# First 512 tokens of a fused attention and MLP block in pairs of token tiles, row maxima sent from ScalarE's queue, output loads spread, scratch of q and k in two parts

## The chip, the cores and the metric

The kernel runs on one core of a Trainium2 chip. The metric is device time in microseconds of one execution, the median over runs. A core has a matrix engine (TensorE, PE in the profile), VectorE (DVE), ScalarE (ACT), GpSimd (POOL) and SyncE (SP), each with an instruction queue of its own that it works off in order, and 16 DMA engines, for which the queues of SP, ScalarE and GpSimd can issue transfers.

## What is computed

The reference adds an attention block and a gated MLP to the input, both fed by the same layer norm of x. There are 2048 tokens of width 512, 32 heads of width 16, and a hidden width of 2 x 896. Everything is float32.

```python
def _A_ref(x, wqkv, wo):
    qkv = (x @ wqkv).reshape(B, S, 3, H, Dh).transpose(2, 0, 3, 1, 4)
    q, k, v = qkv[0], qkv[1], qkv[2]
    scores = jnp.einsum("bhqd,bhkd->bhqk", q, k) * (Dh ** -0.5)
    p = _softmax(scores, axis=-1)
    o = jnp.einsum("bhqk,bhkd->bhqd", p, v)
    return o.transpose(0, 2, 1, 3).reshape(B, S, D) @ wo

def _B_ref(x, w_in, w_sp, b_sp, w_out):
    z = _gelu(jnp.einsum("bsd,df->bsf", x, w_in))
    z1 = z[..., :Fh]
    z2 = _layernorm(z[..., Fh:], axis=-1)
    g = jnp.einsum("ts,bsf->btf", w_sp, z2) + b_sp[None, :, None]
    return jnp.einsum("bsf,fd->bsd", z1 * g, w_out)

xn = _layernorm(x, axis=-1)
return x + _A_ref(xn, wqkv, wo) + _B_ref(xn, w_in, w_sp, b_sp, w_out)
```

## The kernel before

**Numbers in two parts.** Every factor of a float32 product is kept as a high part, rounded to the reduced format fp32r, and a low part, the rest. `mm3` (L161) makes a product of three matmuls, high x high, low x high and high x low, at lines L162 to L164. `split` (L157) makes the parts of an input: ScalarE copies it to the rounded high part (`act`, L55; its instruction is L57 for every copy, exponential and tanh that goes through it), VectorE subtracts that from the input (L159). Weights are fetched by `begin` (L168) and split by `end` (L182). By default GpSimd makes both parts, at L187 and L188. With `early`, which only the preamble uses, GpSimd's own queue loads the weight a second time, straight into the tile of the high part (L179), and VectorE makes the low part (L185).

**Layout.** `x` comes in four chunks `g` of 512 tokens, each of four token tiles of 128. `load_x` (L223) fetches a chunk as two tiles of 128x1024, each holding a pair of token tiles. `norm_x` (L233) is a generator: VectorE takes statistics of each token tile (L244, L245), ScalarE the root of the variance (L247), VectorE the reciprocal and the shift, and ScalarE scales each token tile (L253); with `parts=2` it does the chunk in two halves. `turn_x` (L255) transposes a chunk on PE (L259), four 128x128 blocks for each of the four blocks `c` of the model width, into a PSUM tile of the tag `s`, of which there are three; then it splits that into `xnT[g, c]` and stores it to DRAM for later stages. The tags `d` and `o` of PSUM have one tile each and hold the products.

**Preamble (L816 to L855).** Before the steady loop the instructions are issued in the written order. `x` of chunk 0, the weights of q and k for the first eight heads (`w0`, called wqk0_0 and wqk0_1), `x` of chunk 1 and the four blocks of the weights of v (`wv`) are loaded; chunk 0 is normalized and turned whole. Then, for each chunk, `qk_group` (L287) makes q and k of the first heads (24 products), `load_stacks` (L598) loads them back from DRAM, and `v_tile` (L334) makes v for the chunk's four token tiles (12 products each); the next chunk's normalization and transposes are put between these. So chunk 0's order is 16 transposes, q, k, v0 to v3.

**q and k through DRAM.** `qk_split` (L305) splits a block of q or k, and `qk_store` (L278) writes it to `qscr` or `kscr` in three parts for 512 tokens: for q high, low, high, for k high, high, low, so that one part is written twice, in two DMAs of 512 KB and 256 KB. `load_stacks` then copies the three parts of 16 rows each of a head in one DMA to 48 partitions of `qst` and `kst`, which puts the three products of scores into one matmul of 48 rows. There are 16 pairs `p` of heads, `NP`; `qst` and `kst` have two buffers, used in turn.

**Steady loop.** A counter `half` runs in half-steps. A step is three attention tiles `b`, `b + 1`, `b + 2` of 128 keys by 512 queries for two heads: `scores` (L903 is its matmul) fills a PSUM tile of tag `s`, `exp` on ScalarE (tile `pf`, of which there are `PF` = 6) makes the probabilities, and `pv` multiplies them with v (L877) into the tag `o`. `LEAD` = 27 tiles ahead of it the row maxima are made: `max_mm` (L630) computes scores of queries by keys, `max_red` (L638) reduces them on VectorE, and once per 16 tiles `max_fin` (L641) ends the maximum of 512 queries: VectorE transposes it into `ms` (L657), SP sends `ms` to DRAM (`mscr`), and four DMAs bring it back as rows of `qst`, so that the score matmul subtracts the maximum itself. There are 64 such maxima. `half` starts at -18, so that the first nine steps, the lead-in, have maxima only; attention starts at `b` = 0.

**Background work.** PE's remaining time is filled from `queue`: the rest of q and k, the second half of the hidden layer (`z2_all`) with its layer norm on GpSimd, the first half (`z1_all`), the product over tokens (`spatial`), the output of the MLP (`mlp_out`, L564, which loads two parts of the hidden product, `hp`, and a tile of `x`, `xr`, one token tile ahead) and the output of attention (`attn_out`). A `credit` (L993) says how many ns of background products may be issued at the end of a half-step: 2600 in each half-step of the lead-in, four products of three matmuls; from `b` = 0 on, in odd half-steps only, a share of the work that is left.

**Queues and delays.** `move` (L100) issues a DMA from SP. `later(k, ...)` keeps a call for `k` half-steps, and `flush` issues what is due at the head of a half-step. `store` issues at once from GpSimd's queue in the preamble and through `later` on SP in the steady loop. An estimate of when GpSimd will be free, `pool[0]` (L110 to L123), in a time of 2.7 us per half-step, decides when a generator goes on after work on GpSimd (`pool_done`); whatever is given to GpSimd adds to it, the preamble's work too. Buffers are tiles of a pool that are used in turn; a DMA into a buffer, or out of one, stands at the head of its queue until its data are there.

## Time and profile before

| | us |
|---|---|
| runs of the kernel before | 1963.83, 1964.72, 1965.18 (median 1964.72) |
| the profiled execution | 1965.23 |
| its span, first to last instruction | 1963.1 |
| busy: TensorE (PE) | 1933.9 (99%) |
| busy: VectorE | 1372.9 (70%) |
| busy: ScalarE | 1231.7 (63%) |
| busy: GpSimd | 720.9 (37%) |

The span is what the trace covers; the time of the profiled execution has 2.13 us beside it. The engines' busy times overlap. Mean granted clock of TensorE over the span was 0.997 of full speed. A row of the order of time has the start in the span, the duration (of one instruction, or from the first to the last of a run of like ones), the engine, the line, the operation, the output and input tiles with their sizes, and, in brackets, the engine's idle time just ahead of it and what ended it. A row of a group has the line, the engine, the operation and the count, then least, median and greatest ns of one, then the first and last start. A row of a stretch has its bounds and length, then each engine's busy time with its count of instructions. A row of the waits has the engine with the waiting instruction, the engine and instruction that ended the waits, and their sum, count and longest in us.

### The profile page before, as it was taken

To read this page: it belongs to the slowest core of one execution; us is meant where nothing else is said; L and a number is where in the kernel's file an instruction comes from. 1 tells how busy PE (TensorE), PEld (TensorE's weight loads), DVE (VectorE), ACT (ScalarE), POOL (GpSimd) and SP (SyncE) were. 2 spreads that over 40 slices of the span, in tenths; PEclk is the share of its full clock that TensorE was granted. 3 is DMA by queue.
4 is the path that set the end of the run, shared out by engine and by line. 5 is a ranking of instruction groups with operands and counts; after the bars stand their busy time and mean duration, and the time that the engine had idled before them with its cause. 6 is when DMAs were issued, how large, how long until landed. Compare 5 with 4: busy or idle time off the path is not lost.

```text
span 1963.1 us, 32545 instructions
## 1 busy us (share of the span) xinstructions
PE 1933.9 (99%) x12544; PEld 1047.0 (53%) x12544; DVE 1372.9 (70%) x1562; ACT 1231.7 (63%) x1402; POOL 720.9 (37%) x787
## 2 busy tenths in 40 slices
PE   7999999999999999999999999999999999999998
PEld 6765555555555555555555555555555555555543
DVE  5256777777777677777777777777777777777872
ACT  4336778888777665656666665665566655556664
POOL 2234368789776931026122531017112300002100
PEclk9999999999999999999999999999999999999999
DMA  9586444363535645365545744346364645355323
GB/s 327 204 292 200 139 107 122 108 176 111 154 117 159 187 123 140 91 162 159 151 138 154 211 129 125 108 126 204 105 163 135 176 142 145 106 152 154 105 73 113
DMA packets 234195, 294.20 MB, mean 150 GB/s; under 512 B 34536, under 2 KB 134520, under 8 KB 231160
## 3 DMA queue, kind: packets, MB, share of 16 engines
q1 hardware_dynamic: 229816, 282.08, 49.4%
q0 software_dynamic: 4224, 10.04, 1.4%
q8 instruction: 99, 1.62, 0.3%
q14 instruction: 56, 0.46, 0.1%
HBM read 190.09 MB, written 101.97 MB: 149 GB/s over the span
## 4 chain that ended last, share of the span: by engine, by line
PE 91%; DVE 3%; POOL 2%; DMA 2%; ACT 1%; issue 1%; SPq 0%; DVEq 0%; POOLq 0%; ACTq 0%
PE o L877 23%; PE mx L630 15%; PE st L903 15%; PE sp L162 7%; PE sp L164 5%; PE sp L163 5%; PE mo L162 2%; PE z1p L162 2%; PE qk L162 1%; DVE mm L638 1%; PE mo L163 1%; PE mo L164 1%; PE z2p L162 1%; PE z1p L164 1%; PE z1p L163 1%; PE qk L163 1%
## 5 line engine op out<-in xcount | busy, mean ns | idle before, releaser
L638 DVE TENSOR_REDUCE mm<-mx 128x2 f32<-128x1024 f32 x1024 | 1221.5, 1222 | 501.3 <-PE mx L630 497.2
L57 ACT ACTIVATE pf<-st 128x1024 f32<-128x1024 f32 x1024 | 1028.7, 1025 | 621.9 <-PE st L903 597.2
L877 PE MATMUL o<-pf,vall 128*32 128x512 f32 (+1 forms) x5120 | 511.0, 513 | 0.0
L630 PE MATMUL mx<-kst,qst 48*128 48x512 f32 x2048 | 446.9, 434 | 3.1 <-DVE mm L638 2.0
L903 PE MATMUL st<-qst,kst 50*128 50x512 f32 x2048 | 445.6, 432 | 1.5 <-DVE mm L638 1.4
L630 PEld LDWEIGHTS mx<-kst,qst 48*128 48x128 f32 x2048 | 192.0, 185 | 268.7 <-ACT pf L57 168.6
L903 PEld LDWEIGHTS st<-qst,kst 50*128 50x128 f32 x2048 | 193.3, 185 | 164.0 <-issue 85.7
L877 PEld LDWEIGHTS o<-pf,vall 128*32 128x32 f32 x5120 | 131.4, 109 | 233.7 <-issue 211.7
L162 PE MATMUL sp<-wsp,zs 128*128 128x512 f32 x448 | 193.8, 433 | 0.3 <-DVE z1i L549 0.2
L556 POOL TENSOR_TENSOR z1i<-z1i,hhl 128x512 f32<-128x512 f32 x28 | 36.0, 1286 | 425.9 <-DVE z1i L549 422.4
L164 PE MATMUL sp<-wsp,zs 128*128 128x512 f32 x448 | 175.9, 393 | 0.0
L163 PE MATMUL sp<-wsp,zs 128*128 128x512 f32 x448 | 175.9, 393 | 0.0
L162 PEld LDWEIGHTS sp<-wsp,zs 128*128 128x128 f32 x448 | 83.9, 187 | 68.9 <-issue 52.1
L164 PEld LDWEIGHTS sp<-wsp,zs 128*128 128x128 f32 x448 | 84.1, 188 | 19.3
L163 PEld LDWEIGHTS sp<-wsp,zs 128*128 128x128 f32 x448 | 84.4, 188 | 12.2
L187 POOL CAST wo<-wo0r 128x512 fp32r<-128x512 f32 x1 | 0.6, 611 | 191.4 <-DMA wo0r<-in_wo 191.4
L310 POOL TENSOR_TENSOR qkhl<-qr,qkhl 128x512 fp32r<-128x512 f32 x24 | 30.9, 1289 | 78.9 <-ACT qkhl L57 78.8
L162 PE MATMUL z2p<-w,xt 128*128 128x448 f32 x128 | 51.3, 401 | 0.0
L162 PE MATMUL mo<-wout,hp 128*128 128x512 f32 x112 | 48.5, 433 | 0.6 <-DVE xr L593 0.4
L691 POOL TENSOR_TENSOR ob<-ob 128x512 f32<-128x512 f32 (+1 forms) x16 | 20.6, 1288 | 77.0 <-DMA ob<-rscr 54.5
L164 PE MATMUL z2p<-w,xt 128*128 128x448 f32 x128 | 46.9, 366 | 0.0
L163 PE MATMUL z2p<-w,xt 128*128 128x448 f32 x128 | 46.8, 365 | 0.0
(378 smaller groups left out, 1974.8 us busy)
## 6 DMA issues: line engine op xcount, KB each, us to landing
zs<-z2scr SPq DMA_DIRECT2D x112, 512.0 KB
escr<-e SPq DMA_DIRECT2D x60, 256.0 KB
hscr<-hhl SPq DMA_DIRECT2D x28, 512.0 KB
qst<-qscr SPq DMA_DIRECT2D x30, 384.0 KB
kst<-kscr SPq DMA_DIRECT2D x30, 384.0 KB
xscr<-xnT POOLq DMA_DIRECT2D x16, 512.0 KB, 6.0
qscr<-qkhl SPq DMA_DIRECT2D x16, 512.0 KB
kscr<-qkhl SPq DMA_DIRECT2D x16, 512.0 KB
```

Source lines behind the costliest of these rows:

```text
L57: return nc.scalar.activation(out, in_, func, **kw)
L162: nc.tensor.matmul(acc, lh, rh, start=first, stop=False)
L163: nc.tensor.matmul(acc, ll, rh, start=False, stop=False)
L164: nc.tensor.matmul(acc, lh, rl, start=False, stop=last)
L187: gps(0.6).tensor_copy(t[:, 0, :n], rw[:, :n])
L310: gps(1.3).tensor_sub(hl[:, 1, :], src, hl[:, 0, :].bitcast(F32))
L556: gps(1.3).tensor_add(z1, z1, hl[:, 1, :].bitcast(F32))
L630: nc.tensor.matmul(acc[:, j, :], qst[p % 2][rows, tt * P:(tt + 1) * P], kst[p % 2][rows, kc * 512:(kc + 1) * 512], start=True, stop=True)
L638: dve(1024).tensor_reduce(mmax[i // 16][:, :, t, kc], mstep.pop(i), AX.X, ALU.max)
L691: gps(1.3).tensor_mul(both[rows, 0, :], both[rows, 0, :], both[rows, 2, :])
L877: nc.tensor.matmul(acc[cols:cols + VW, a:a + w], vpack(kt - 1 + r, 2 * p + j), pf[:, j * 512 + a:j * 512 + a + w], start=(kt == 1 and a == ...
L903: nc.tensor.matmul(st[:, j, :], kst[p % 2][rows, kt * P:(kt + 1) * P], qst[p % 2][rows, c * 512:(c + 1) * 512], start=True, stop=True)
```

## The change

*The start.* `x` of chunk 0 is loaded as four DMAs of one token tile each. The weights of v come next, then those of q and k, then chunks 1 and 2 of `x`. GpSimd's second loads of the weights are gone (`early` now chooses only the buffer). For wv0 and wv3 ScalarE copies the high part and VectorE subtracts; wv1, wv2 and `w0` are split by GpSimd. `norm_x` yields between its two halves, and `turn_x` takes a range of token tiles: tiles 0 and 1 are turned first (eight transposes in one go, then four splits of half width), then v0 is made, and v1 turns tiles 2 and 3 after its sixth product through `mid`; v2 and v3 follow. Chunk 1 is normalized between these tiles. q and k of chunk 0 come after its v instead of before, and chunk 1 is turned right after the first q. In later chunks too `turn_x` issues all 16 transposes before the first split, with blocks 0 and 3 sharing one PSUM tile. A root of `epst` on ScalarE, whose result is overwritten, stands first.

*GpSimd's estimate* is set back to -1000 at the end of this part, so the work given to GpSimd until then no longer counts.

*Maxima.* `ms` is sent to DRAM by ScalarE's queue instead of SP's, right after the exponentials of the next half-step, through the list `behind`; the four row loads stay on SP, two half-steps after the transpose.

*Output loads.* In `mlp_out` the two `hp` loads are issued one and two half-steps later and `xr` three, except for the first token tile.

*Scratch.* `qscr` and `kscr` keep two parts, for q high and low, for k low and high, stored by one DMA of 512 KB; `load_stacks` takes the three parts of a head with two DMAs, one of two parts and one of the third.

*Credit.* At `b` = 0 each half-step in which no product with v was issued gets the credit of the lead-in, 2600.

```diff
-    qscr = [dr.tile([P, 3, S], F32, name=f"qscr{m}") for m in range(4)]
-    kscr = [dr.tile([P, 3, S], F32, name=f"kscr{m}") for m in range(4)]
+    qscr = [dr.tile([P, 2, S], F32, name=f"qscr{m}") for m in range(4)]
+    kscr = [dr.tile([P, 2, S], F32, name=f"kscr{m}") for m in range(4)]
     xscr = [[dr.tile([P, 2, 512], F32, name=f"xscr{g}_{c}") for c in range(ND)] for g in range(NG)]
...
+    def soon(k, fn, *args):
+        fn(*args)
+
     def flush():
...
         rw = t512(nm + "r") if early == "t" else big.tile([P, 512], F32, tag="raw", name=nm + "r", bufs=3)
-        dst, hi = rw[:, :n], t[:, 0, :n]
+        dst = rw[:, :n]
         if blocks > 1:
             src = src.rearrange("(c p) f -> p c f", p=P)
-            dst, hi = (v.rearrange("p (c f) -> p c f", c=blocks) for v in (dst, hi))
+            dst = dst.rearrange("p (c f) -> p c f", c=blocks)
         move(dst, src)
-        if early:
-            nc.gpsimd.dma_start(hi, src)
         return t, rw, n
-    def end(loaded, early=False):
+    def end(loaded, low=None, high=False):
         t, rw, n = loaded
-        if early:
-            nc.vector.tensor_sub(t[:, 1, :n], rw[:, :n], t[:, 0, :n].bitcast(F32))
+        if high:
+            low.tensor_sub(t[:, 1, :n], rw[:, :n], t[:, 0, :n].bitcast(F32))
+        elif low:
+            nc.scalar.activation(t[:, 0, :n], rw[:, :n], AF.Copy)
+            low.tensor_sub(t[:, 1, :n], rw[:, :n], t[:, 0, :n].bitcast(F32))
         else:
...
         for i in range(len(xt)):
-            k = 4 // len(xt)
+            k = 2
             t = 4 * g + k * i
-            rows = x[t * P:(t + k) * P, :]
-            move(xt[i], rows if k == 1 else rows.rearrange("(a p) d -> p a d", p=P))
             for j in range(k):
-                xs[g, k * i + j] = xt[i] if k == 1 else xt[i][:, j, :]
+                xs[g, k * i + j] = xt[i][:, j, :]
+            if g == 0:
+                for j in range(k):
+                    move(xt[i][:, j, :], x[(t + j) * P:(t + j + 1) * P, :])
+                    yield
+            else:
+                move(xt[i], x[t * P:(t + k) * P, :].rearrange("(a p) d -> p a d", p=P))
...
             tiles = range(a * k, (a + 1) * k)
+            if a:
+                yield
             sl = slice(a * k, (a + 1) * k)
...
-    def turn_x(g):
+    def turn_x(g, lo=0, hi=4):
+
+        tiles = [spsum(f"xT{g}_{lo}_{c}") for c in range(3)]
+        sl = slice(lo * P, hi * P)
         for c in range(ND):
-            pt = spsum(f"xT{g}_{c}")[:, 0, :]
-            for i in range(4):
-                nc.tensor.transpose(pt[:, i * P:(i + 1) * P], xs[g, i][:, c * P:(c + 1) * P], ident)
-            t = piece(f"xnT{g}_{c}")
-            split(t[:, 0, :], t[:, 1, :], pt, 512)
-            store(xscr[g][c], t)
-            xnT[g, c] = t
+            for i in range(lo, hi):
+                nc.tensor.transpose(tiles[c % 3][:, c // 3, i * P:(i + 1) * P], xs[g, i][:, c * P:(c + 1) * P], ident)
+        for c in range(ND):
+            if lo == 0:
+                xnT[g, c] = piece(f"xnT{g}_{c}")
+            t = xnT[g, c]
+            split(t[:, 0, sl], t[:, 1, sl], tiles[c % 3][:, c // 3, sl], (hi - lo) * P)
+            if hi == 4:
+                store(xscr[g][c], t)
...
-
-    def qk_store(scr, order, hl, sl, first=False):
-        put = move if first else store
-        r = 1 if order[0] == order[1] else 0
-        put(scr[:, r:r + 2, sl], hl)
-        put(scr[:, 2 - 2 * r, sl], hl[:, 0, :])
...
         hl = hilo(f"qkhl{m}_{a}_{g}")
-        act(hl[:, 0, :], src, AF.Copy, 512)
+
+        act(hl[:, a, :], src, AF.Copy, 512)
         yield
         if m:
-            gps(1.3).tensor_sub(hl[:, 1, :], src, hl[:, 0, :].bitcast(F32))
+            gps(1.3).tensor_sub(hl[:, 1 - a, :], src, hl[:, a, :].bitcast(F32))
             yield from pool_done()
         else:
-            dve(512).tensor_sub(hl[:, 1, :], src, hl[:, 0, :].bitcast(F32))
-        qk_store((qscr, kscr)[a][m], ((0, 1, 0), (0, 0, 1))[a], hl, slice(g * 512, (g + 1) * 512), m == 0)
+            dve(512).tensor_sub(hl[:, 1 - a, :], src, hl[:, a, :].bitcast(F32))
+        (store if m else move)((qscr, kscr)[a][m][:, :, g * 512:(g + 1) * 512], hl)
         yield
...
-    def v_tile(t, ws):
+    def v_tile(t, ws, mid=None):
         acc = dpsum(f"v{t}", "do"[t % 2])
...
         for c in range(ND):
+            if c == 2 and mid:
+                mid(t + 1)
             xt = xnT[t // 4, c]
...
                 h = piece(f"hp{t}_{i}")
-                move(h[:, :, :n * P].rearrange("p a (f q) -> p a f q", q=P), hscr[t // 4][:, :, t % 4, 4 * i:4 * i + n, :])
+                (later if t else soon)(i + 1, move, h[:, :, :n * P].rearrange("p a (f q) -> p a f q", q=P), hscr[t // 4][:, :, t % 4, 4 * i:4 * i + n, :])
                 hp.append(h)
             xt = t512(f"xr{t}")
-            move(xt, x[t * P:(t + 1) * P, :])
+            (later if t else soon)(3, move, xt, x[t * P:(t + 1) * P, :])
             return hp, xt
...
             for i, (t, scr) in enumerate(((q, qscr), (k, kscr))):
-                args = t[64 * j:64 * j + KS, cols], scr[m][sl[j], :, cols]
-                if p and 2 * j + i:
-                    later(2 * j + i, move, *args)
-                else:
-                    move(*args)
+                two = t[64 * j:64 * j + 2 * DH, cols], scr[m][sl[j], :, cols]
+                one = t[64 * j + 2 * DH:64 * j + KS, cols], scr[m][sl[j], i, cols]
+                for args in (two, one):
+                    if p and 2 * j + i:
+                        later(2 * j + i, move, *args)
+                    else:
+                        move(*args)
     NSTEP = NP * 64
+    behind = []
     mstep = {}
...
         load["D"] += 0.6
-        later(1, move, mscr[g % 4].rearrange("b k x -> (b k) x"), ms)
+        behind.append((now[0] + 1, mscr[g % 4].rearrange("b k x -> (b k) x"), ms))
         for j in range(2):
...
     with tc.manual_schedule(engines=engines):
-        load_x(0)
-        w0 = [begin(*qk_weights(0, a), early="t") for a in range(2)]
-        load_x(1)
-        ones = big.tile([P, 512], F32, tag="raw", name="ones", bufs=3)
-        nc.vector.memset(ones[0:32, 0:P], 1.0)
+        nc.scalar.activation(mhalf, epst, AF.Sqrt)
+        nc.vector.memset(mhalf, -0.5)
+        first = load_x(0)
+        next(first)
+        next(first)
         wv = []
...
             wv.append(begin(f"wv{c}", wqkv[c * P:(c + 1) * P, 2 * D:3 * D], 512, t=t, early="rt"[c % 2]))
+            if c == 0:
+                run(first)
+        w0 = [begin(*qk_weights(0, a), early="t") for a in range(2)]
+        run(load_x(1))
+        run(load_x(2))
+        ones = big.tile([P, 512], F32, tag="raw", name="ones", bufs=3)
+        nc.vector.memset(ones[0:32, 0:P], 1.0)
+        norm = norm_x(0, 2)
+        next(norm)
+        nc.scalar.activation(wv[0][0][:, 0, :], wv[0][1], AF.Copy)
+        next(norm)
+        wv[0] = end(wv[0], nc.vector, True)
+        next(norm)
+        wv[1:3] = [end(l) for l in wv[1:3]]
+        turn_x(0, 0, 2)
+        wv[3] = end(wv[3], nc.vector)
         nc.gpsimd.dma_start(cscr.rearrange("o (a b) -> (o a) b", b=P), ones[0:16, 0:P])
...
         nc.gpsimd.memset(vall[:, NT * H * (DH + 1):], 0.0)
-        run(norm_x(0, 2))
-        load_x(2)
-        w0 = [end(l, True) for l in w0]
-        turn_x(0)
-        load_x(3)
+        w0 = [end(l) for l in w0]
+        run(norm)
+        v_tile(0, wv)
+        v_tile(1, wv, lambda t: turn_x(0, 2, 4))
+        norm1 = norm_x(1, 2)
+        next(norm1)
+        v_tile(2, wv)
+        next(norm1)
+        next(norm1)
+        v_tile(3, wv)
+        run(norm1)
+        run(load_x(3))
         init_rows(0)
-        wv = [end(l, True) for l in wv]
-        norm = norm_x(1, 2)
+        pool[0] = -1000.0
         for g in range(NG):
+            once = True
             for y in qk_group(0, g, w0, ("d", "o")):
-                if y == 0 and g == 0:
-                    next(norm, 0)
+                if y == 0 and once and g < 2:
+                    once = False
+                    if g == 0:
+                        turn_x(1)
+                        norm = norm_x(2)
+                    else:
+                        next(norm)
             load_stacks(0, slice(g * 512, (g + 1) * 512))
...
                     wq[1, a] = end(wq[1, a])
-            for t in range(4 * g, 4 * g + 4):
+            for t in range(4 * g, 4 * g + 4) if g else ():
                 next(norm, 0)
...
                 tiles.insert(1 if half % 2 == 0 else 2 * i, (max_mm, m))
+            before = done
             for make, n in tiles:
...
                 exp(n)
+            while behind and behind[0][0] <= half:
+                nc.scalar.dma_start(*behind.pop(0)[1:])
             for f in final:
...
             ready += len(ns)
-            if b < 0:
+            if b < 0 or b == 0 and done == before:
                 credit = 2600
```

## The prediction

> **What bounds the kernel now.** I read the first page, then the stretches of 25 us, then the order of time at the start, and last the waits. The head of the page and four of the stretches (length, then the busy time of PE, weight loads, VectorE, ScalarE and GpSimd, the granted clock, the DMA share, GB/s):
>
> ```profile
> span 1963.1 us, 32545 instructions
> PE 1933.9 (99%) x12544; PEld 1047.0 (53%) x12544; DVE 1372.9 (70%) x1562; ACT 1231.7 (63%) x1402; POOL 720.9 (37%) x787
> ...
> 0.00:25.00 25.00, 15.48 (x64) 12.26 (x65) 15.59 (x40) 11.81 (x20) 10.21 (x23) 1.00 1.04 344
> 125.00:150.00 25.00, 22.37 (x96) 14.81 (x96) 13.11 (x11) 11.56 (x17) 9.02 (x7) 0.94 0.90 327
> 425.00:450.00 25.00, 24.18 (x165) 12.60 (x162) 18.52 (x24) 20.68 (x26) 19.50 (x29) 1.00 0.61 178
> 1950.00:1975.00 25.00, 3.97 (x38) 1.18 (x36) 6.38 (x7) 0.38 (x1) 0.00 (x0) 0.81 0.23 85
> ```
>
> PE bounds it. Of 1963.1 us PE is idle 29.2: 9.5 in the first 25 us, 2.6 between 125 and 150, 0.8 between 425 and 450, and 9.1 in the last stretch (its 13.1 us less 3.97), which the edits leave alone. PE issues the same matmuls and as many transposes after the change, so the change can win or lose only in such gaps, in the clock, or by new ones. The profiled execution took 1965.23 us, 2.13 beyond its span; the runs' median is 1964.72. The sum starts from 1965.23.
>
> **The start in pairs.** These rows of the order of time price it; the row of 33.50 is the first product of the second chunk, the common mark up to which both versions do the same PE work (32 transposes, 72 products).
>
> ```profile
> 4.54 0.69 DVE L244 BATCH_NORM_STATS2 bst<-x 128x6 f32<-128x512 f32 x1 [3.46 <-DMA x<-in_x]
> 6.07 0.18 DVE L245 BATCH_NORM_AGGREGATE mv<-bst 128x2 f32<-128x6 f32 x1
> 6.28 0.30 ACT L247 ACTIVATE rs<-mv,epst 128x2 f32<-128x2 f32 x1 [4.27 <-DVE mv L245]
> 7.01 1.52 ACT L253 ACTIVATE x<-x,rs 128x512 f32<-128x512 f32 x2 [0.43 <-DVE rs L249]
> 10.91 3.04 PE L259 MATMUL xT<-ident,x 128*128 128x128 f32 x13 [0.23 <-ACT x L253]
> 11.43 0.60 ACT L57 ACTIVATE xnT<-xT 128x512 fp32r<-128x512 f32 x1 [0.57 <-PE xT L259]
> 13.60 0.63 PE L162 MATMUL qk<-xnT,wqk 128*128 128x512 f32 x1
> 25.80 1.20 PE L259 MATMUL xT<-ident,x 128*128 128x128 f32 x9 [0.28 <-ACT x L253]
> 33.50 0.39 PE L162 MATMUL qk<-xnT,wqk 128*128 128x512 f32 x1
> ...
> L57 ACT ACTIVATE e<-o x1: 384/384/384, 1951.3 to 1951.3; 128x256 f32<-128x256 f32 x1
> L187 POOL CAST wqk<-wqk_0r x3: 612/613/622, 68.2 to 97.4; 128x512 fp32r<-128x512 f32 x3
> L188 POOL TENSOR_TENSOR wqk<-wqk_0r,wqk x3: 1289/1291/1293, 68.9 to 98.1; 128x512 fp32r<-128x512 f32 x3
> ```
>
> A pair of token tiles (512 KB) landed before 4.54. One tile is 0.262 MB, 0.76 us at 344 GB/s, so the first tile alone comes at 3.8, the second at 4.5, and each later 256 KB 0.7 after the one ahead of it, GpSimd's six own loads being gone: wv0 5.2, tiles 2 and 3 at 5.9 and 6.6, wv1 to wv3 at 7.3, 8.0, 8.7. The statistics of two tiles took 1.71 (4.54 to 6.25) and end at 5.5; but ScalarE's queue now has wv0's copy ahead of the root (0.6, from 5.2), so the root starts at 5.8, the scaling 0.73 later (6.28 to 7.01), and tile 1 is scaled at 8.1 against 8.53 before. Eight transposes follow instead of sixteen, at 0.23: 9.7. The first split waits for all eight, because the fourth block shares a tile with the first: 9.9, plus 0.38, and **the first product starts at 10.3 instead of 13.60**.
>
> Then the inputs are traced along v0. GpSimd makes wv1 and wv2 (1.9 each) by 9.2 and 11.1; wv3's copy stands behind four splits on ScalarE (11.9), its low part is out at 12.6. The array is still slow: a transpose takes 0.23 (3.04 / 13) at 11, 0.13 (1.20 / 9) at 26, and a product at half clock 0.43 (rows further down) instead of 0.23. At 0.43, v0 reaches its last block at 14.1, so no input holds it long. Tiles 2 and 3 wait behind wv3's copy for their root and are scaled at 14.45. If the full clock comes at 13.1, 18 products end at 15.7; eight transposes make it 16.8, and 42 products (half of v1, v2, v3, the first of q) 26.3. Chunk 1 is ready only at 26.6: its scalings on ScalarE stand behind the evictions of v2 and v3. Sixteen transposes and 12 products of k end at 31.4, against 33.50: **-2.1**. Bounds: full clock already at 11.4, -3.0; not before all 18, +0.2. I take 13.1, since before a stretch of 2.7 us of transposes was enough (10.91 to 13.60).
>
> **Transposes later.** Before, the fourth block waits for a free tile, here in chunks 2 and 3:
>
> ```profile
> 46.45 0.66 PE L259 MATMUL xT<-ident,x 128*128 128x128 f32 x4 [0.59 <-DVE xnT L159]
> 65.38 0.66 PE L259 MATMUL xT<-ident,x 128*128 128x128 f32 x4 [0.59 <-DVE xnT L159]
> ```
>
> That wait goes (three tiles hold four blocks). What is late next: chunk 2's statistics move behind the second chunk's q, 3.4 us on VectorE, and its scalings end 1.0 us after v5. So -0.59 in chunk 3 and +0.4 in chunk 2: **-0.2** (from -1.2 to +0.5).
>
> **Scratch in two parts; the first maximum.** Each store of q and k falls from 768 KB in two issues to 512 KB in one, 32 of them.
>
> ```profile
> 117.01 0.32 SPq L101 DMA_DIRECT2D mscr<-ms  x1
> 136.18 0.63 ACT L57 ACTIVATE qkhl<-qr 128x512 fp32r<-128x512 f32 x1 [7.16 <-DMA kscr<-qkhl]
> 137.35 0.50 PE L162 MATMUL qk<-xnT__1182,wqk 128*128 128x512 f32 x1 [1.55 <-ACT qr L57]
> ```
>
> SP stood at the first maximum until 117.01 with a store of q behind it; a later store was slow at 327 GB/s, ScalarE waited 7.16 for its buffer and PE 1.55. After, that store is ahead of the row loads in SP's queue and six such stores carry 1.6 MB less, some 5 us at that rate. **-1.55** (bounds -1.55 and 0). The stacks' loads become twice as many of the same bytes; 0.43 us of issue each on SP, 60 more over 1800 us, far ahead of their use: 0.
>
> **More background work at step 0.** Here PE passes to scores and exponentials:
>
> ```profile
> 144.50 1.94 ACT L57 ACTIVATE pf<-st 128x1024 f32<-128x1024 f32 x2 [0.61 <-PE st L903]
> 146.00 0.50 PE L630 MATMUL mx<-kst,qst 48*128 48x512 f32 x2 [1.08 <-DVE mm L638]
> 146.33 0.60 ACT L57 ACTIVATE qr<-qk 128x512 f32<-128x512 f32 x1
> 146.98 0.75 PE L162 MATMUL qk<-xnT__1182,wqk 128*128 128x512 f32 x1
> 148.00:150.00 2.00, 2.00 (x7) 1.15 (x7) 0.90 (x1) 0.55 (x1) 1.00 (x1) 0.50 0.06 23
> 148.38 0.63 PE L162 MATMUL qk<-xnT__1184,wqk 128*128 128x512 f32 x1
> 148.81 0.63 PE L163 MATMUL qk<-xnT__1184,wqk 128*128 128x512 f32 x1
> ```
>
> Before, PE idles 1.08, then six products run at a granted clock of 0.50, 0.43 apart (148.38 to 148.81): 1.2 lost. The built order puts 12 products right behind the second score tile, 12 more behind the third. The first 12 need ScalarE's copy (146.33), queued behind two exponentials, so PE idles from 144.9 to 146.98, 2.1; the next 12 need a copy behind the third exponential: 1.0 + 0.6 less 0.4 of matmuls, 1.2. So 3.3 idle instead of 1.08; the 18 products done early are not lost. With full clock +1.0, with the same half clock as before +2.2; I take the middle, **+1.6** (bounds 0, if the copy comes in time, and +3.6, two such windows).
>
> The Trainium skill, TensorE: Matmul & The Clock Gate, What's actually happening, puts the fall to half clock after at least one idle window of about 3.4 us. Here 1.08 us of idle sufficed, so the row disagrees; by that rule the term would be +1.0 and the result 1962.4.
>
> **Maxima by ScalarE.** 64 issues leave SP and stand in ScalarE's queue behind the third exponential; ScalarE's next exponential, hence PE, waits for each.
>
> ```profile
> L101 SPq DMA_DIRECT2D mscr<-ms x64: 314/326/627, 117.0 to 1907.9; - x64
> 1012.10 0.21 DVE L657 STREAM_TRANSPOSE ms<-mrow 128x32 f32<-128x32 f32 x1
> 1012.75 1.02 ACT L57 ACTIVATE pf<-st 128x1024 f32<-128x1024 f32 x1 [0.63 <-PE st L903]
> 1015.67 1.02 ACT L57 ACTIVATE pf<-st 128x1024 f32<-128x1024 f32 x1 [1.90 <-PE st L903]
> 1883.00 2.16 ACT L57 ACTIVATE pf<-st 128x1024 f32<-128x1024 f32 x2 [0.56 <-PE st L903]
> SPq L101 <- DVE ms L657: 210.8, 58, 15.4
> PE mo L162 <- DVE xr L593: 0.4, 2, 0.2
> ```
>
> The transpose is done at 1012.31, ScalarE reaches the issue at 1013.77 and is idle 1.90 before its next exponential; the least such idle time is 0.56 (1883.00). An issue of 0.33, SP's price, fits. It also waits for an earlier SP transfer on its semaphore, in the built order mostly six or more steps back: 0. **0**, from -2.5 (SP free of 210.8 us of waiting, the gap of 425 to 450 and its like closed) to +20.5 (63 x 0.326 uncovered). The row loads follow 1.5 us later, eleven steps of 1.8 us ahead of use. Output loads spread by one to three half-steps: a tile lasts about five of them, and PE waited 0.4 us for such tiles in all: 0.
>
> Sum: 1965.23 - 2.1 - 0.2 - 1.55 + 1.6 = **1963.0**.
>
> **The rivals.** *Everything lands (B).* The full clock comes early (-3.0), chunk 2 loses nothing (-1.2), the lead-in is clean (-1.55), step 0 costs 0 to 1, SP's freedom closes 1: some -6, 1959.5. For it: the DMA engines were full for 38 us and lose 1.5 MB; against: ScalarE stands in the way at four places above. *ScalarE's queue decides (C).* If an issue takes longer than the idle before the next exponential (from 0.56; mostly 1.2 to 1.9), every maximum delays PE. If 0.33 shows in each: 1963.0 + 20.5 = 1983.5; in a third of them, 1970. Against: the rows above. *The start moves its stall (D).* The array stays slow through all of v0 and v1 (+2.3 on the forecast) and two windows at half clock at step 0 (+2.0): 1967.3, still no change. *The stage of 300 to 500 us (E).* GpSimd is busy 19.50 of 25 at 425 to 450; the shifted order makes SP's stores, and through its semaphore ScalarE, wait on it. Two waits of 3.5: 1970.
>
> **How the numbers follow.** Forecast 0.40 (own range 1960 to 1966.5), B 0.32, C 0.12, D 0.08, E 0.08. About 0.2%, 3.9 us, is what a measurement can tell from no change: 1960.8 to 1968.6 counts as none. Faster: B and the fifth of the forecast that lies below 1960.8, 0.40. Within: the rest of it and D, 0.40. Slower: C and E, 0.20. The range 1957.5 to 1970.5 leaves out C's upper part and the far end of B, and takes in E.
>
> **What would show it.** First product near 10.3, second chunk's q near 31.4; no PE gap of 1.55 before the scores, but gaps near 2.1 and 1.2 at them; ScalarE's issues without waits, PE idle near 27 in all. A PE total that falls by over 5, or exponentials that start late after each maximum, would prove me wrong.

## The result, and the profile after

| | before | changed |
|---|---|---|
| median of 6 runs (us) | 1964.95 | 1976.27 |
| lowest to highest | 1963.83 to 1967.53 | 1973.53 to 1979.70 |
| ratio, 95% interval | | 1.0057 (1.0047 to 1.0067) |

The change made the kernel 11.3 us slower, against a forecast of 1963.0. The profiled execution of the changed kernel is the slowest of its six, 1979.7, so what follows from its trace adds up to 3.4 us more than the median shows. The head of its page:

```profile
span 1977.8 us, 32600 instructions
PE 1943.4 (98%) x12544; PEld 1050.2 (53%) x12544; DVE 1374.6 (70%) x1565; ACT 1233.8 (62%) x1409; POOL 722.1 (37%) x785
```

Its stretches, with columns as in the prediction:

```profile
0.00:25.00 25.00, 15.70 (x65) 12.54 (x66) 11.62 (x36) 11.89 (x24) 13.83 (x25) 1.00 0.83 293
125.00:150.00 25.00, 21.57 (x90) 14.45 (x89) 10.62 (x10) 10.84 (x17) 7.72 (x6) 0.93 0.90 317
425.00:450.00 25.00, 23.80 (x129) 13.30 (x121) 15.50 (x17) 16.94 (x22) 16.84 (x28) 0.81 0.37 111
```

PE does the same 12544 matmuls, yet it is busy 9.5 us longer (1943.4 against 1933.9) and idle 5.2 us longer (34.4 against 29.2). Together that is the 14.7 us by which the span grew. Longer busy with the same work means a slower clock, and the third of the stretches shows it: 0.81 where it was 1.00. Narrow stretches hold nearly all of it:

```profile
144.00:148.00 4.00, 4.00 (x14) 2.71 (x14) 0.00 (x0) 0.00 (x0) 1.06 (x1) 0.57 0.96 334
424.00:434.00 10.00, 9.10 (x36) 5.13 (x32) 3.72 (x5) 4.16 (x5) 5.20 (x11) 0.51 0.63 193
1670.00:1674.00 4.00, 4.00 (x24) 1.61 (x17) 1.81 (x4) 1.57 (x2) 0.00 (x0) 0.57 0.44 134
```

A mean clock of 0.57 over 4 us is 3.4 us at half clock; the three add up to 16.7 us, and half of that, 8.4, is time lost. (The second goes on a little: from 434 to 435 the clock is 0.73.) Each stands right behind a wait of PE. The view of PE's waits of the changed kernel (releaser, sum, times, longest):

```profile
PE xT L271 <- ACT x L263: 9.2, 3, 8.7
PE st L946 <- DVE mm L653: 5.8, 10, 1.3
PE qk L165 <- ACT qr L57: 3.4, 2, 2.1
PE mx L645 <- DVE mm L653: 2.2, 3, 0.9
PE mx L645 <- ACT pf L57: 2.2, 3, 1.7
```

The same view of the kernel before:

```profile
PE mx L630 <- DVE mm L638: 2.0, 2, 1.1
PE st L903 <- DVE mm L638: 1.4, 5, 0.4
```

Scores (`st`) wait for reductions ten times instead of five, 5.8 us instead of 1.4, and the copy of q (`qr`) holds PE up for 3.4. Two of the waits of scores are 1.32 long, at scores 154 and 853. This is the second, in the order of time, behind a step of ordinary shape:

```profile
1662.15 0.51 PE L946 MATMUL st<-qst,kst 50*128 50x512 f32 x2
1662.49 0.40 PE L645 MATMUL mx<-kst,qst 48*128 48x512 f32 x2
1662.73 0.40 PE L946 MATMUL st<-qst,kst 50*128 50x512 f32 x2
...
1667.44 0.51 PE L645 MATMUL mx<-kst,qst 48*128 48x512 f32 x2
1667.98 1.23 DVE L653 TENSOR_REDUCE mm<-mx 128x2 f32<-128x1024 f32 x1 [0.60 <-PE mx L645]
1669.27 0.50 PE L946 MATMUL st<-qst,kst 50*128 50x512 f32 x2 [1.32 <-DVE mm L653]
```

In the ordinary step the second score follows its maximum within 0.24 us. In the other it starts 0.06 after the reduction of *that same maximum*. The built program says why: of the three PSUM tiles of tag `s`, maximum 878, maximum 879 and score 853 were all given the same one, while the tile of score 851 stood next in turn for maximum 879. Which of the three a new tile takes is settled when the program is built. A place is out of turn when a score or a maximum got another tile than the next in the cycle of three. In the kernel before, 12 places are out of turn and none reuses the tile used just before; in the changed kernel there are 25, and two such reuses, exactly scores 154 and 853.

To see the rest, I took for both kernels the start of each score and subtracted the background products already done (0.2345 us each, 0.2055 for those 448 wide), so that work merely moved does not count. The difference to the kernel before, in us:

```
score   time   after  e1     e9     e7     e13    e14    e10
0       143.9  -3.95  -3.46  -5.28  -3.75  -4.42  -3.16  -0.02
16      171.1  -1.44  -2.53  -6.81  -5.25   0.75  -4.28   2.49
64      257.1  -0.18  -1.63  -2.04  -5.27   1.00  -3.97   3.51
144     402.9   0.26  -1.30  -2.14  -5.53   1.55  -2.18   3.97
160     430.1   6.75  -1.87  -2.15  -5.51   1.57  -0.87   3.36
192     490.0   8.88  -0.51  -2.16  -5.48   1.65  -1.49   4.62
272     630.2   8.67  -0.69  -2.18  -5.48   1.48  -1.75   4.42
288     659.2  10.92   1.33  -1.82  -5.38   1.62  -0.91   4.42
848    1647.3  12.05   2.36   2.75  -4.68   2.53   2.77   5.73
864    1676.5  15.19   2.31   4.29  -4.71   2.50   2.76   5.73
1023   1947.2  15.08   2.26   4.09  -4.66   2.74   2.78   5.47
```

(The column "time" is the score's start before. e1 to e14 are the experiments below, numbered as they were run, so that the seventh run is e7; each column is one execution.) The changed kernel gains 3.95 up to the first score, as the prediction wanted, and loses 19 afterwards: 2.5 at the first sixteen scores, 6.5 around score 154, 3.1 at score 853, and most of the rest in pieces between 200 and 720 us.

### The profile page after: what moved, and what is told of

Same layout as the page of the kernel before. It is cut to its first block, busy times and chain, and to the rows that moved or that the text cites. A ratio compares the mean times of both kernels' runs of the same rounds, so it can differ in the third digit from the quotient of the medians.

```text
span 1977.8 us, 32600 instructions
## 1 busy us (share of the span) xinstructions
PE 1943.4 (98%) x12544; PEld 1050.2 (53%) x12544; DVE 1374.6 (70%) x1565; ACT 1233.8 (62%) x1409; POOL 722.1 (37%) x785
## 4 chain that ended last, share of the span: by engine, by line
PE 86%; DVE 3%; DMA 1%; ACT 1%; issue 1%; POOL 1%; SPq 0%; DVEq 0%; ACTq 0%; POOLq 0%
PE o L920 23%; PE st L946 15%; PE mx L645 15%; PE sp L165 7%; PE sp L167 5%; PE sp L166 5%; DVE mm L653 2%; PE mo L165 2%; PE z2p L165 2%; PE z1p L165 1%; PE mo L166 1%; PE mo L167 1%; PE z2p L167 1%; PE z2p L166 1%; PE z1p L167 1%; PE z1p L166 1%
```

## The experiments

Three theories stood. Theory 1: the order of the PSUM tiles. Theory 2: ScalarE's queue is held up by the 64 issues of the maxima, which now wait there for transfers. Theory 3: the credit at `b` = 0 puts the background work in a worse phase. Each run has its own runs of the kernel before on the same chip, with medians of 1965.8 to 1966.0.

### Tiles strictly in turn

The three tiles get a tag each, used in turn; nothing else changes.

```diff
+    turns = [0]
+
     def spsum(nm):
 
-        return ps.tile([P, 2, 512], F32, tag="s", name=nm, bufs=3)
+        turns[0] = (turns[0] + 1) % 3
+        return ps.tile([P, 2, 512], F32, tag=f"s{turns[0]}", name=nm, bufs=1)
```

> The changed kernel with the three PSUM tiles of tag s handed out strictly in turn (three tags with one tile each). Theory 1 (tile order: the time is lost where a score or maximum got the tile of the maximum just before it, or another tile out of turn, and waits for that reduction): the waits of 1.32 us at scores 154 and 853 and the half clock behind them go, and with them most of the smaller ones; 1960 to 1966 us, PE idle 27 or less. Theory 2 (ScalarE's queue: the issue of the maxima delays the exponentials): within 3 us of the changed kernel's 1976. Theory 3 (the credit at b = 0 puts the background work of 150 to 500 us in a worse phase): also near 1976.

Measured (e1): 1968.76 (1966.32 to 1971.07), ratio 1.0015 (1.0006 to 1.0024). The waits at 154 and 853 are gone and 7.5 us with them, so theory 1 holds for most of the loss, but the rest misses its range. The waits that are left in its profiled run (span 1964.6, the clock at 1.00 in every stretch of 1 us up to 1957):

```profile
PE xT L274 <- ACT x L266: 8.9, 3, 8.4
PE qk L168 <- ACT qr L57: 3.4, 2, 2.1
PE st L949 <- DVE mm L656: 3.0, 9, 0.5
PE mx L648 <- ACT pf L57: 2.8, 4, 1.4
```

> The kernel before with the same three tiles handed out strictly in turn. Theory 1: 12 places out of turn go, among them the wait of 1.08 us at maximum 28; 1961 to 1964 us. Theories 2 and 3: no change from 1965, within 1 us.

Measured (e2): 1964.93 (1963.51 to 1965.88), ratio 0.9995 (0.9986 to 1.0003). The kernel before loses nothing that can be told by its 12 places, against the 1961 to 1964 of theory 1. So a place out of turn is not yet a cost; what the changed kernel has and this one has not is the reuse of the tile used just before.

### The scratch, alone and undone

The fourth run puts the scratch in two parts into the kernel before, with the new store and the new loads of the stacks; the third takes the same lines out of the changed kernel. Tiles as the build hands them out.

```diff
-    qscr = [dr.tile([P, 3, S], F32, name=f"qscr{m}") for m in range(4)]
+    qscr = [dr.tile([P, 2, S], F32, name=f"qscr{m}") for m in range(4)]
...
-                args = t[64 * j:64 * j + KS, cols], scr[m][sl[j], :, cols]
+                two = t[64 * j:64 * j + 2 * DH, cols], scr[m][sl[j], :, cols]
+                one = t[64 * j + 2 * DH:64 * j + KS, cols], scr[m][sl[j], i, cols]
...
```

> The changed kernel with the scratch of q and k and its loads as before (three parts, two stores, one load for each 48 rows); the built program then has 13 places out of turn instead of 25 and no score on the tile of the maximum just before it. Theory 1: 1961 to 1967 us. Theories 2 and 3: 1973 to 1979.

> The kernel before with the scratch in two parts alone; its built program has 25 places out of turn, 4 of them on the tile used just before. Theory 1: 1970 to 1978 us, with waits of over 1 us at scores 31 and 340. Theories 2 and 3: 1961 to 1965.

Measured (e3, then e4): 1969.19 (1966.14 to 1972.72) and 1969.90 (1967.53 to 1975.26), ratios 1.0021 (1.0012 to 1.0030) and 1.0024 (1.0015 to 1.0033). The first lies above theory 1's range and the second 0.1 below its own; both are far from what theories 2 and 3 expected. The first gives the same as tiles in turn: seven of the eleven us. The second makes the kernel before 4.1 us slower with one edit, and its waits of 1.2 to 1.3 us stand at the scores (31, 340) and maxima (761, 953) that its built program names:

```profile
PE st L906 <- DVE mm L641: 4.1, 7, 1.3
PE mx L633 <- ACT pf L57: 3.5, 8, 1.2
```

So the scratch in two parts, whose loads I costed at nothing, brings the disorder: the build hands out the tiles otherwise. Whether the doubled loads do it or the stores, now one in place of two, was not separated.

> The changed kernel with its PSUM tiles in turn and with the scratch in three parts as before. What is left of the loss in the first run (1968.8 against 1965.8) may come from twice as many stack loads ahead of the spatial weights in SP's queue: then 1966 to 1967, without the wait of 1.4 us at maximum 313. If the scratch cost only through the tile order: 1968 to 1969.5.

Measured (e5): 1969.26 (1967.83 to 1971.04), against 1968.76 with two parts: nothing more to win from the scratch once the tiles are in turn. The wait at maximum 313 did go, though, and this is how it arises in the changed kernel, a chain over two engines:

```profile
POOL wsp L191 <- DMA wsp_0r<-in_w_spT: 2.5, 1, 2.5
```

That row is from the waits between 640 and 672 us; the next two are from the order of time:

```profile
668.38 0.63 ACT L57 ACTIVATE z<-z 128x512 f32<-128x512 f32 x1 [3.16 <-POOL z L359]
669.97 0.50 PE L645 MATMUL mx<-kst,qst 48*128 48x512 f32 x2 [1.73 <-ACT pf L57]
```

A weight of the product over tokens arrives late, GpSimd waits 2.5 for it, its next work for the gelu is late, ScalarE stands 3.16 at the tanh, the exponentials behind it are late, and PE idles 1.73. What the run wins there it lost before its first score (-1.38 against -3.46 in e1).

### The maxima and the output loads

```diff
-        behind.append((now[0] + 1, mscr[g % 4].rearrange("b k x -> (b k) x"), ms))
+        later(1, move, mscr[g % 4].rearrange("b k x -> (b k) x"), ms)
```

> The changed kernel with its PSUM tiles in turn and the maxima sent by SP again. If ScalarE's 64 issues cost what their waits show (some 2 us over the run): 1966 to 1967. If they cost nothing, or SP's own waits cost as much: 1968 to 1969.5.

Measured (e6): 1967.32 (1965.97 to 1973.07). It lies between the two expectations, 1.4 us from e1 with a spread of 7: not decided here. The same edit on a base with less spread, with the old credit (below):

> The seventh run's kernel (PSUM tiles in turn, old credit, 1959.35) with the maxima sent by SP again. If ScalarE's issues are hidden in its idle time, as the prediction had it: within 1 us of 1959.35. If SP's freedom is what closes small gaps: 1960.5 to 1962. If ScalarE's issues cost: below 1958.5.

Measured (e11): 1959.13 (1958.29 to 1960.37) against 1959.35. With the old credit theory 2 falls. The Trainium skill, DMA: Bandwidth & Descriptors, Issuing engines are not separate DMA queues, says that issuing from more engines saves only the time of the issue itself; these two medians agree. In the changed kernel ScalarE does wait behind its issues for earlier transfers, but little:

```profile
ACT pf L57 <- DMA mscr<-ms: 4.9, 4, 1.9
```

In e7 the same row has 6.8 in four waits, and e11 shows that they cost nothing. In e1 it has 14.8 in nine; with the new credit the issues may cost up to the 1.4 us of e6.

```diff
-                (later if t else soon)(i + 1, move, h[:, :, :n * P].rearrange("p a (f q) -> p a f q", q=P), hscr[t // 4][:, :, t % 4, 4 * i:4 * i + n, :])
+                soon(i + 1, move, h[:, :, :n * P].rearrange("p a (f q) -> p a f q", q=P), hscr[t // 4][:, :, t % 4, 4 * i:4 * i + n, :])
```

The load of `xr` is issued at once likewise.

> The seventh run's kernel (PSUM tiles in turn, old credit, 1959.35) with the output loads issued together as before. If the spreading is worth nothing, as the prediction had it: within 1 us of 1959.35. If it matters, PE waits before output products return and it takes 1960.5 or more.

Measured (e12): 1959.36 (1957.85 to 1960.51): the spreading is worth nothing.

### The start

The second run's kernel with the lines of the change's diff for `begin`, `end`, `load_x`, `norm_x`, `turn_x`, `v_tile` and the preamble, and none for scratch, maxima, output loads and credit.

> The kernel before with its PSUM tiles in turn and the new start alone (pairs of token tiles, the new order of loads, GpSimd's estimate set back; scratch, maxima, output loads and credit as before). The start gains 2.3 us up to the first maximum in the changed kernel's trace: 1962 to 1963. If it gives back later what it wins: 1964.5 to 1966.

Measured (e8): 1961.55 (1960.33 to 1965.55), 3.4 below the second run and just below the range expected, ratio 0.9981 (0.9973 to 0.9990): the gain stays. The run doesn't separate the transposes and GpSimd's estimate from the rest of the start, and its profiled execution, 1964.72, is the slowest but one of eleven. With the scratch in three parts PE still stands before the first score here:

```profile
PE qk L168 <- ACT qr L57: 1.8, 1, 1.8
```

### The credit

```diff
-            if b < 0 or b == 0 and done == before:
+            if b < 0:
                 credit = 2600
```

> The changed kernel with its PSUM tiles in turn and without the credit at b = 0. If the background work at step 0 costs the 2.1 and 1.4 us of idle PE that the trace shows in place of 0.7 to 1.1, and puts the later stages in a worse phase: 1964 to 1966.5. If the work done early pays for it: 1968 to 1970.

Measured (e7): **1959.35** (1959.02 to 1961.14), ratio 0.9970 (0.9959 to 0.9981), below both expectations and faster than both kernels. With the tiles in turn one condition costs 9.4 us. PE's waits now:

```profile
PE xT L274 <- ACT x L266: 8.5, 3, 8.0
PE mx L648 <- ACT pf L57: 1.8, 7, 0.7
PE st L949 <- DVE mm L656: 1.1, 4, 0.4
```

> The changed kernel with the old credit at b = 0 alone; PSUM tiles as the build hands them out, here with 5 scores or maxima on the tile used just before (scores 31, 340, 853, maxima 506, 761). Two causes that add: 1959.35 of the seventh run plus five waits of 1.2 to 1.3 us, 1965 to 1967, with PE idle before those five and the small losses between 200 and 700 us gone. If the credit were the cause only together with the tile order: 1960 or below. If the tile order were the larger cause: above 1969.

Measured (e9): 1968.58 (1967.35 to 1971.03), above the range. The five waits stand where the built program has them. By the column e9 the one at score 31 costs most, 4.8 (from -6.81 to -2.04):

```profile
193.40 0.49 PE L946 MATMUL st<-qst,kst 50*128 50x512 f32 x2 [1.32 <-DVE mm L653]
```

And the stretch behind it:

```profile
194.00:202.00 8.00, 8.00 (x42) 4.06 (x38) 2.80 (x3) 2.82 (x3) 3.60 (x5) 0.57 0.77 230
```

1.32 of idle, then 6.9 us at half clock (8.00 at 0.57), 3.4 of them lost. All that follows, with the other four waits in it, costs 6.1, and behind those four the clock doesn't fall. The table of the two causes, in us:

```
                  new credit   old credit
tiles as built     1976.27      1968.58
tiles in turn      1968.76      1959.35
```

Each cause costs 7.5 to 9.4 whether the other is there or not (the kernel before had 1964.95 beside the first of the four, 1965.8 to 1965.9 beside the others).

> The kernel before with its PSUM tiles in turn (1964.93 in the second run) and with the credit at b = 0 alone. If that credit costs what the first and seventh runs show, 9.4 us, whatever else is changed: 1972 to 1976. If it costs only the idle PE at step 0: 1965.5 to 1967.5. If it does harm only beside the other edits: within 1 us of 1964.93.

Measured (e10): 1971.90 (1970.15 to 1974.29), ratio 1.0032 (1.0019 to 1.0044): 7.0 above the second run and 0.1 below the first range. The credit does its harm in the kernel before as well.

Why it costs so much more than the idle time at step 0 was still open. Two kernels took it apart: one gives the lead back at once, one makes the lead without touching step 0.

```diff
+            elif half == 2 * (3 // 3) + 1:
+                credit = credit + 1843 - 3900
             elif half % 2:
```

> The changed kernel with its PSUM tiles in turn and with the new credit at b = 0, but the 18 products that run ahead are given back at once (credit reduced by 3900 at b = 3), so that from score 9 on the background stands as with the old credit. If the loss of 9.4 us lies in the background standing 12 to 18 products ahead through the stages of 200 to 720 us: 1960.5 to 1963 (1959.35 and the idle PE at step 0, 1 to 2.4). If it lies in step 0 and the half clock there: 1967 to 1969.

Measured (e13): 1969.92 (1966.70 to 1971.26), above both ranges. By its number step 0 would be the cause, but the column e13 of the table says more: it has lost 5.2 by score 16 (-4.42 to 0.75), 0.9 more by 192 and 1.1 more in all that follows. Paying back made idle PE of its own, because without background products the scores wait for the reductions:

```profile
154.53 0.50 PE L949 MATMUL st<-qst,kst 50*128 50x512 f32 x2 [0.69 <-DVE mm L656]
155.45 0.50 PE L648 MATMUL mx<-kst,qst 48*128 48x512 f32 x2 [0.42 <-ACT pf L57]
159.38 0.49 PE L949 MATMUL st<-qst,kst 50*128 50x512 f32 x2 [0.85 <-DVE mm L656]
160.51 0.49 PE L949 MATMUL st<-qst,kst 50*128 50x512 f32 x2 [0.40 <-DVE mm L656]
```

These four come to 2.4, and right behind them the clock falls, 3.4 us at half clock (4.00 at 0.57):

```profile
161.00:165.00 4.00, 4.00 (x24) 1.45 (x24) 1.31 (x2) 1.27 (x2) 0.00 (x0) 0.57 0.40 104
```

So this run doesn't price step 0 by itself. What it does show: with no lead, the stages from 257 to 720 us lose next to nothing. The other kernel's edit:

```diff
-            if b < 0 or b == 0 and done == before:
+            if b < 0:
                 credit = 2600
+            elif half % 2 and b in (9, 12, 15):
+                credit = credit + 1843 + 2600
```

> The changed kernel with its PSUM tiles in turn and the old credit at b = 0, but 2600 more credit at each of b = 9, 12 and 15, so that the background stands 12 to 18 products ahead from score 15 on, as with the new credit, without its idle time at step 0. If the lead costs: 1964 to 1968. If step 0 costs: 1959 to 1960.5.

Measured (e14): 1968.49 (1965.57 to 1972.97), 0.5 above the range of the lead. Without the idle time of step 0 the lead costs 9 us. In the trace this lead is larger than the one it stands for: 24 products between scores 24 and 100, and it shrinks later. Its column loses nearly all after score 16, mostly in small pieces; the largest, 1.15 at score 544, is by the profile a wait for the rows of a maximum from DRAM. One kind of piece, from the first run, shows the phase:

```profile
243.56 0.21 DVE L675 STREAM_TRANSPOSE ms<-mrow 128x32 f32<-128x32 f32 x1
243.69 1.11 DVE L391 BATCH_NORM_STATS2 zst<-z 128x6 f32<-128x448 f32 x2
244.97 3.44 DVE L656 TENSOR_REDUCE mm<-mx 128x2 f32<-128x1024 f32 x3
246.19 0.50 PE L949 MATMUL st<-qst,kst 50*128 50x512 f32 x2 [0.43 <-DVE mm L656]
...
247.32 0.50 PE L949 MATMUL st<-qst,kst 50*128 50x512 f32 x2 [0.39 <-DVE mm L656]
```

The statistics of a layer norm, 1.11 us, fall on VectorE right behind the end of a maximum. The reductions start late, and two scores wait 0.43 and 0.39. With the background 12 to 18 products further, such meetings come about; the seventh run has no wait at these scores. That the other pieces arise in this way is not shown.

What is shown is that the credit costs 7 to 9 us, in both kernels. How that divides between step 0 and the lead stays open. By score 16 the column e1 stands 2.7 behind e7; at the end it stands 6.9 behind, and 1.9 of that comes with the wait at maximum 313. e13, without the lead, is as slow as e14, without the idle time of step 0. So a rival stands untested: the old credit's order may happen to be a good one, and any other start of the background work worse.

## Why the prediction was wrong

**The start: right, with the parts mis-sized.** The order of time of the changed kernel:

```profile
6.46 0.63 ACT L849 ACTIVATE qst<-wv0r 128x512 fp32r<-128x512 f32 x1 [4.24 <-DMA wv0r<-in_wqkv]
7.00 0.28 ACT L257 ACTIVATE rs<-mv,epst 128x2 f32<-128x2 f32 x1
11.51 0.80 PE L165 MATMUL v<-qst,xnT 128*128 128x512 f32 x1 [0.47 <-ACT xnT L57]
...
14.27 0.60 PE L165 MATMUL v<-kst,xnT 128*128 128x512 f32 x1
14.69 0.41 PE L166 MATMUL v<-kst,xnT 128*128 128x512 f32 x1
14.94 0.39 PE L167 MATMUL v<-kst,xnT 128*128 128x512 f32 x1
...
32.18 0.39 PE L165 MATMUL qk<-xnT,wqk 128*128 128x512 f32 x1
...
85.46 0.50 PE L645 MATMUL mx<-kst,qst 48*128 48x512 f32 x2
```

The first product starts at 11.51, not 10.3: ScalarE waited for wv0 until 6.46, where I had 5.2, and the root stood behind it. Full speed came at about 14.7, where I had 13.1: up to there the products are 0.43 apart, then 0.23 to 0.25. The common mark is at 32.18, not 31.4, so -1.3 in place of -2.1. The transposes gave what was missing, -1.0 where I had -0.2. In the kernel before the first maximum is this row:

```profile
87.76 0.50 PE L630 MATMUL mx<-kst,qst 48*128 48x512 f32 x2
```

It came 2.30 earlier in the changed kernel. That this is the sum of my two terms, -2.1 and -0.2, is luck: each was 0.8 off, and the errors cancel. By itself the start is worth 3.4 between medians (e8).

**The scratch at the first maximum: right.** The first score starts at 143.94 in the kernel before and at 139.98 in the changed one:

```profile
143.94 0.50 PE L903 MATMUL st<-qst,kst 50*128 50x512 f32 x2
139.98 0.50 PE L946 MATMUL st<-qst,kst 50*128 50x512 f32 x2
```

It came 3.95 earlier, 1.65 more than the first maximum; forecast 1.55. With the new start and three parts, in e8, PE still waits 1.8 there.

**The scratch's loads at 0: the first step that failed.** "The stacks' loads become twice as many of the same bytes; 0.43 us of issue each on SP [...] far ahead of their use: 0." On SP that holds but for the wait at maximum 313, which the scratch in two parts has with the new credit (e1) and in three parts has not (e5). But the scratch in two parts changed which of the three PSUM tiles scores and maxima take, and that costs 7.5 to 9.2 us (the columns of the table of two causes; 5.0 in the kernel before, e4 against e2). The prediction took it that PE issues the same matmuls, which is so, and left out which tiles they write to, which the built program settles. Why the edit changes the build's choice was not tried.

**Step 0: the idle time right, what follows wrong.** I worked out gaps of 2.1 and 1.2, and they are 2.07 and 1.36:

```profile
143.03 0.50 PE L165 MATMUL qk<-xnT__1194,wqk 128*128 128x512 f32 x1 [2.07 <-ACT qr L57]
149.88 0.50 PE L165 MATMUL qk<-xnT__1194,wqk 128*128 128x512 f32 x1 [1.36 <-ACT qr L57]
```

The term was +1.6 with bounds 0 and +3.6; the table has +2.5 by score 16. The step that failed is "the 18 products done early are not lost", as if nothing followed from them. They are not lost, but they leave the background 12 to 18 products ahead up to some 700 us. From score 16 on the column e1 loses 4.8 us and e14 7.1, where e7, with the old credit, loses 0.6. The whole term, +1.6 in the sum, measures 7.0 to 9.4 between medians; why the lead costs so much is shown in one place only and stays open for the rest.

**Maxima at 0 and output loads at 0: right,** by e11 and e12, both with the old credit. There ScalarE's idle time does cover the issues.

**The rivals.** E named the stage of 300 to 500 us, where the changed kernel loses 8.6 (scores 144 to 192, from 0.26 to 8.88), but for another reason than it gave, SP's stores behind GpSimd with ScalarE behind them: ScalarE's waits behind its issues add up to 4.9 in the whole run, and most of the 8.6 stands at score 154. Nothing in the prediction stood for the disorder of the tiles or for the price of the lead, so its range ended at 1970.5. Without both, in e7, the kernel takes 1959.35; the sum without the +1.6 of step 0 is 1961.4.

**The clock.** The prediction priced a fall of the clock from one row, 3.4 us at half clock. That held at 144 and 1670; at 424 there were some 10 in one piece, and 6.9 in e9. The Trainium skill, TensorE: Matmul & The Clock Gate, What's actually happening, has the fall come after an idle window of some 3.4 us; here idle PE of 1.32 us sufficed at scores 154, 853 and 31, while 1.32 at scores 340 and 853 of e9, and 2.07 and 1.37 in e1, left the clock whole. The length of one fall, 3.4, agrees with its window. The Trainium skill, Perfetto Trace Analysis, Matmuls, says that independent groups of matmuls should go around different PSUM banks, so that reading one out overlaps the next; scores 154 and 853 show the price when they don't.

## What to carry to other kernels

Where a pool hands out PSUM tiles when the program is built, compare the tiles too, not only the order of the instructions: an edit far away (here how q and k are kept in DRAM) can put a matmul on the tile that is just being read, and one tag for each tile, used in turn, takes the question away. Work done early on an engine that is full need not be free: here a credit that put some 18 products ahead went with a loss of 7 to 9 us, much of it spread over the stretch in which the lead lasted, so price it over that stretch. And test the parts of a change one by one: this one held two edits worth nothing, a start that gained 3.4 us, a scratch that gained 1.6 in one place and lost 7 to 9 in another, and a credit that lost 7 to 9; with tiles in turn and the old credit it takes 1959.35.

## What the runs showed that was not expected

A wait of PE of 1.32 us costs far more than itself when the clock falls behind it: 3.4 us at half clock behind score 853, 6.9 behind score 31 in e9, some 10 behind score 154. Longer waits at other moments cost no clock at all (e1). What decides it these runs don't show. The kernels with many such waits also spread more, 6 us between the lowest and the highest of the changed kernel against 2.1 in the seventh run. The mean granted clock, which is on record for each execution, goes with it: 0.998 in the changed kernel's fastest (1973.53) and 0.994 in its slowest (1979.70), 0.999 and 0.997 in those of e1, 0.999 and 0.996 in those of e14, but 0.998 to 0.999 in all six of the seventh run. So a part of what the medians of e1 and e14 lose is the clock, which doesn't fall in their profiled executions while PE works; the columns show 6.9 of the 9.4 between e1 and e7, and 7.4 of the 9.1 between e14 and e7.
